# Sparse attention and a top-2 mixture of experts on one core: the ACT and DVE steps of early list parts take their batch's rank, and experts' products are owed 0.7 instead of 1.0 of the attention's time on TensorE

## The chip, the cores and the metric

The kernel runs on one core of a Trainium2 chip. The metric is device time in microseconds of one execution, the median of three. The page and the trace are of one further execution, taken by the hardware profiler.

## The reference, cut to what matters

```python
# attention: 8 batches, 8 heads, 576 tokens, head size 64; heads 0-3 local, 4-7 strided
scores = scale * np.matmul(q, k.transpose(0, 1, 3, 2))
mask_local = (rel >= 0) & (rel < 32)
mask_strided = (rel >= 0) & (pos[None, :] % 32 == pos[:, None] % 32)
attn = softmax(where(masks, scores, -1e9)); x = matmul(attn, v) -> (4608, 512)
# experts: 8 of them, each token goes to the best two
noisy_logits = x @ w_gate + log1p(exp(x @ w_noise)) * noise
top2 = argpartition(-noisy_logits, 2)[:, :2]; top2_w = softmax of the two logits
for e in range(8):
    for k in range(2):
        mask = top2[:, k] == e
        h = np.maximum(x[mask] @ w1[e], 0.0)          # 512 -> 1024
        out[mask] += top2_w[mask, k, None] * (h @ w2[e])   # 1024 -> 512
```

The second half depends on the first through `x`: which tokens an expert gets is known only batch by batch, as the attention of a batch ends and its tokens are routed.

## The kernel before

**Attention.** The work is cut into 32 units, four to a batch: two pairs of strided heads and two of local heads, in turn. A unit transposes k and q on TensorE (L505, L509), forms two score tiles (masks L550, 36 score products at L557), takes the row maxima on DVE (L584) and the exponentials on ACT (L588, L590), transposes these (L598), multiplies by v (L617, L622), scales on DVE (L627 to L646), and transposes the result for the router (L684, L688) while SP stores it to `x_dram` (L663). Evacuations of PSUM go to ACT or DVE, whichever is free sooner (`copy`, L283 to L287).

**Routing.** After the four units of a batch, `route` runs the gate products (L734), softplus, the best two of eight, and the places in the experts' lists (L785 to L798); GpSimd then writes twelve groups of entries to the lists `tab` in DRAM (L824).

**Experts.** An expert's list is worked off in jobs, two or three blocks of 128 tokens at a time. For the first three experts some jobs are cut so that they need only the batches 0 to hb-1 (`SUBS`, hb below 8): these are the *early list parts*. The first needs two batches, the next two need four, then five, and the last three seven. A job loads its list (`tabt`, L925), GpSimd makes indices (`gix`, L982) and gathers the tokens' rows (`xg`, L966), TensorE transposes them (L1008), ACT rounds them to `xhi` (L1019) and DVE takes the remainder `xlo` (L1021). Layer 1 is eight groups of twelve products (L1050), each followed by a ReLU on ACT (`hhi`, L1069) and a remainder on DVE (`hlo`, L1074). Layer 2 is 24 products of 512 columns for each block (L1116), then DVE weighs the result (`prev`, L1141 or L1143) and GpSimd scatters it to the output (L1150). The weights are loaded as `wraw` and split by ACT (L896) and DVE (L897).

**Order.** The program's order is set before it runs, by a planner (`issue_all`). Each piece of work has an engine, an estimated length and a rank. At every step the planner takes, on each engine, the pieces that could start within 120 ns of the first that could, and of these the one of lowest rank. Attention units have ranks 10u; routing comes with its batch; experts' pieces have ranks from ER = 1,000,000 on, so they come last wherever something else could start. `turn(n)` gives a job with hb below 8 the rank 20·2·(hb-1)+20, that of the middle of its last batch. Before the change only the loads of its lists, its weights' loads and its gathers have that rank. Each engine then works its instructions off in the order that the planner left, whatever their real lengths.

**Owing.** While attention is left and an expert's product could run, each attention piece on TensorE adds PACE times its length to `owed`, each expert's product takes its length off. As long as `owed` is positive, TensorE prefers an expert's product that could start within 120 ns. With PACE = 1.0 that aims at equal shares.

Of the kernel before, what the change touches and what calls it, by code (L numbers as in the profile page):

```python
# [22 lines left out]
def kernel(  # L23
# [13 lines left out]
    B, H, S, D = q.shape  # L37
# [169 lines left out]

    GAP = 1500

    PACE = 1.0  # L210

    class Slot:
        def __init__(self, ring=None):
# [57 lines left out]
    def act(n):  # L271
        return 60 + 0.84 * n

    def dve(n):
        return 75 + 1.04 * n
# [15 lines left out]
    def issue_all(expert_banks, t_start):  # L291
# [43 lines left out]
        while ready:  # L335
# [62 lines left out]
            if e == "PE":  # L398
                owed = max(-1500.0, owed - d) if o.expert else min(3000.0, owed + PACE * d) if filler[0] else 0.0
            ready.remove(o)  # L400
# [503 lines left out]
    def experts(zero):  # L904
# [5 lines left out]
        def turn(n):  # L910
            hb = jobs[n][1][3]
            return None if hb == B else 20 * NP * (hb - 1) + 10 * NP
# [77 lines left out]
        def transposes(n, rank):  # L990


            e, (start, nb, tail, hb) = jobs[n]
            xh, xl = R["xhi"].new(), R["xlo"].new()
            XH[n] = (xh, xl)
            for i in range(nb + (tail > 0)):
                xs, rows_of = G_[n][2:]
                xg = xs[i]
                rows = 128 if i < nb else tail
                ng = rows // 32  # L1000
                cols = slice(128 * i, 128 * i + rows)
                if hb < B:
                    xr = Slot()

                    def tr(o, xg=xg, xr=xr):
                        xv = xg.t.rearrange("p g c -> p (g c)").rearrange("p (x c) -> p c x", c=ND)
                        for c in range(ND):
                            nc.tensor.transpose(xr.t[:, 128 * c:128 * c + 128], xv[:, c, :], ident)  # L1008
                    Piece("PE", 108 * ND, tr, rank, read=[xg], psum=xr, expert=True)
                else:  # L1010
                    xr = R["xr"].new()
                    Piece("DVE", 8 * rows, lambda o, xg=xg, xr=xr, ng=ng, rows=rows: nc.vector.transpose(  # L1012
                        xr.t.rearrange("p (c x) -> p c x", c=ND)[:, :, :rows].rearrange("p c (g i) -> p g c i", g=ng),
                        xg.t[:, :ng, :].rearrange("p g (i c) -> p g c i", c=ND)), rank, read=[xg], alloc=[xr], expert=True)
                how = "write" if i else "alloc"

                def view(xr=xr, rows=rows):
                    return xr.t.rearrange("p (c x) -> p c x", c=ND)[:, :, :rows]
                Piece("ACT", act(4 * rows), lambda o, view=view, cols=cols: nc.scalar.copy(  # L1019
                    xh.t[:, :, cols], view()), rank, read=[xr], expert=True, **{how: [xh]})  # L1020
                Piece("DVE", dve(4 * rows), lambda o, view=view, cols=cols: nc.vector.tensor_tensor(  # L1021
                    xl.t[:, :, cols], view(), xh.t[:, :, cols].bitcast(F32), ALU.subtract),
                      rank, read=[xr, xh], expert=True, **{how: [xl]})
                if i + 2 < nb + (tail > 0):

                    xs.append(rows_of(i + 2))
# [3 lines left out]
        def half_used(e):  # L1030
            if e not in counts:
                counts[e] = nc.values_load(over[:1, E + 1 + e:E + 2 + e], engines=[mybir.EngineType.PE], min_val=0,
                                           max_val=NTOK)
            return counts[e]

        def layer1(n, f, rank):
            e, (start, nb, tail, hb) = jobs[n]
            width = nb * 128 + tail
            xh, xl = XH[n]
            whi, wlo = W[1, f]  # L1040
            hh, hl = R["hhi"].new(), R["hlo"].new()
            HT[n, f] = (hh, hl)
            ps = Slot()

            todo = [(d, a, c) for d in range(ND) for a, c in ((whi, xh), (whi, xl), (wlo, xh))]

            def products(which, width):
                for m in which:
                    d, a, c = todo[m]
                    nc.tensor.matmul(ps.t[:, :width], a.t[:, 128 * d:128 * d + 128], c.t[:, d, :width], start=(m == 0),  # L1050
                                     stop=(m == len(todo) - 1))

            def mm(o):
                last = len(todo) - 1
                if not tail:
                    return products(range(last + 1), width)

                products([0], width)
                with tc.If(half_used(e) > tail // 2) as used:
                    products(range(1, last), width)  # L1060
                with used.Else():
                    with tc.If(half_used(e) > 0) as some:
                        products(range(1, last), width - tail // 2)
                    with some.Else():
                        products(range(1, last), width - tail)
                products([last], width)
            Piece("PE", 12 * (width / 2.4 + 2.5), mm, rank, read=[xh, xl, whi, wlo], psum=ps, expert=True,
                  after=lengths_known if tail else [])
            Piece("ACT", act(width) + 30, lambda o: nc.scalar.activation(hh.t[:, :width], ps.t[:, :width], AF.Relu), rank,  # L1069
                  read=[ps], alloc=[hh], expert=True)  # L1070
            main = nb * 128

            def low(dst, c0, c1):
                nc.vector.scalar_tensor_tensor(dst, ps.t[:, c0:c1], 0.0, hh.t[:, c0:c1].bitcast(F32), op0=ALU.max,  # L1074
                                               op1=ALU.subtract)

            def lows(o):
                low(hl.t[:, :main], 0, main)
                if tail:

                    low(hh.t[:, width:width + tail], main, width)
            Piece("DVE", dve(main) + (dve(tail) if tail else 0), lows, rank, read=[ps, hh], write=[hh] if tail else [],
                  alloc=[hl], expert=True)
# [15 lines left out]
        def layer2(n, i, rank, pv):  # L1099
# [39 lines left out]
            def weighted(o):  # L1139
                if first:  # L1140
                    nc.vector.tensor_scalar(pv.t, ps.t, tb.t[:, i, 1:2].bitcast(F32), None, op0=ALU.mult)  # L1141
                for r in () if first else range(0, 2 * rows if half else rows, rows):
                    nc.vector.scalar_tensor_tensor(pv.t[:rows, :], ps.t[r:r + rows, :], tb.t[:rows, i, 1:2].bitcast(F32),  # L1143
                                                   pv.t[:rows, :], op0=ALU.mult, op1=ALU.add)
            Piece("DVE", (1 + half) * dve(512), weighted, rank, expert=True,
                  **({"read": [ps, tb], "alloc": [pv], "after": zero[:-(-known // ZC)]} if first else
                     {"read": [ps, tb, pv], "write": [pv]}))
# [13 lines left out]
        for i in range(NF):  # L1161
            W[1, i] = weights_of(jobs[0][0], 1, i, ER, turn(0))
        W2[0] = [weights_of(jobs[0][0], 2, i, ER, turn(0)) for i in range(NF)]
        transposes(0, ER)
        for n, (e, (start, nb, tail, hb)) in enumerate(jobs):
            nb += tail > 0
            others = [x for y in range(E) if y != e for x in out_done[y]]
            rank = ER + 100 * n
            change = n + 1 < NJOB and jobs[n + 1][0] != e
            pvs = {i: previous(n, i, rank, others) for i in range(min(2, nb))}  # L1170
            if n + 1 < NJOB:
                gather(n + 1, rank + 1)
            for f in range(NF):
                layer1(n, f, rank + 2)
            if change:
                for i in range(NF):
                    W[1, i] = weights_of(jobs[n + 1][0], 1, i, rank + 20, turn(n + 1))
            if n + 1 < NJOB:
                transposes(n + 1, rank + 3)
            for i in range(nb):  # L1180
                layer2(n, i, rank + 4 + i, pvs[i])
                if i + 2 < nb:
                    pvs[i + 2] = previous(n, i + 2, rank + 4, others)
            if n + 1 < NJOB:
                W2[n + 1] = W2[n]
                if change:
                    W2[n + 1] = [weights_of(jobs[n + 1][0], 2, i, rank + 21, turn(n + 1)) for i in range(NF)]
# [17 lines left out]
    for u in range(NU):  # L1205
        rank = 10 * u
# [92 lines left out]
```

## Time and profile before

| | |
|---|---|
| three executions | 1097.59, 1098.72, 1097.29 us; median 1097.59 |
| the profiled execution | 1092.48 us, of which the span from first to last instruction is 1090.8 us |
| instructions | 23344, of them 8645 matmul records |
| DVE, ACT, POOL busy | 606.2, 434.4, 544.1 us |
| gate products of the eight batches begin at | 43.8, 76.3, 110.9, 142.2, 171.8, 221.2, 271.1, 324.4 us |

Times in the text are us from the start of the span. A row of a view by stretches names the stretch and its length, and for each engine its busy time and, in brackets, the number of instructions; PEld is the loading of weights into TensorE, PEclk the granted clock as a share of full speed. "Busy" of PE counts modelled ends of pipelined matmuls.

### The profile page before, as it was taken

The numbers are of one execution on the slowest core, as the hardware profiler recorded it, in microseconds if no ns is written. First come the engines' busy times: TensorE is split into PE (matmuls) and PEld (weight loads), VectorE is DVE, ScalarE is ACT, GpSimd is POOL, SyncE is SP. The second block draws the span as 40 slices with busy tenths as digits, with TensorE's granted clock in tenths as the row PEclk, the third lists the DMA queues.
The fourth block names the chain that finished last, engine by engine and source line by source line (L and its number), as shares of the span: only waits on it lengthen the run. The fifth ranks groups of instructions, "written<-read, shape, count | busy, mean of one in ns | idle before, by whom it ended". The sixth has DMA issues, their size and how long they took to land.

```text
span 1090.8 us, 23344 instructions
## 1 busy us (share of the span) xinstructions
PE 1058.4 (97%) x8645; PEld 933.9 (86%) x8645; DVE 606.2 (56%) x1614; ACT 434.4 (40%) x1123; POOL 544.1 (50%) x730
## 2 busy tenths in 40 slices
PE   8888899999999999999999999999999999999995
PEld 7776679888898899889998989898988898898994
DVE  7779896687655235647663455345534653374341
ACT  6789986666653112314331233123311331142120
POOL 1045353434425455656666546564646465647520
PEclk8999999999999999999999999999999999999998
DMA  8889999889454323535553245224522452243210
GB/s 178 206 179 234 231 217 232 222 228 269 132 168 116 100 87 98 152 115 174 171 177 93 71 116 177 79 62 131 163 76 69 126 166 74 78 144 107 73 57 23
DMA packets 169163, 151.89 MB, mean 139 GB/s; under 512 B 52588, under 2 KB 137068, under 8 KB 169029
## 3 DMA queue, kind: packets, MB, share of 16 engines
q1 hardware_dynamic: 145028, 92.30, 33.8%
q0 software_dynamic: 24000, 57.82, 17.4%
q8 instruction: 82, 1.34, 0.5%
q14 instruction: 53, 0.43, 0.1%
HBM read 111.72 MB, written 39.39 MB: 139 GB/s over the span
## 4 chain that ended last, share of the span: by engine, by line
PE 89%; DVE 4%; ACT 3%; DMA 2%; issue 1%; POOL 0%; POOLq 0%; DVEq 0%; ACTq 0%; SPq 0%
PE bankA L1116 6%; PE bankH L1116 6%; PE bankA L1050 5%; PE bankD L1116 5%; PE bankG L1116 5%; PE bankB L1050 5%; PE bankH L1050 5%; PE bankE L1050 5%; PE bankD L1050 5%; PE bankG L1050 5%; PE bankB L1116 5%; PE bankE L1116 4%; PE bankF L1050 4%; PE bankC L1050 4%; PE bankC L1116 4%; PE bankF L1116 3%
## 5 line engine op out<-in xcount | busy, mean ns | idle before, releaser
L973 POOL DMA_INDIRECT xg<-x_dram,gxx x240 | 240.4, 1002 | 111.7 <-issue 56.7
L1150 POOL DMA_INDIRECT out_dram<-prev,tabt x80 | 81.5, 1019 | 104.1 <-DVE prev L1143 51.2
L824 POOL DMA_INDIRECT tab<-ent,addr x96 | 93.1, 970 | 74.8 <-issue 24.7
L1092 POOL DMA_INDIRECT prev<-out_dram,gix x76 | 73.3, 964 | 85.8 <-issue 30.2
L1012 DVE STREAM_TRANSPOSE xr<-xg 128x512 f32<-128x512 f32 (+1 forms) x64 | 66.4, 1038 | 18.1 <-DMA xg<-x_dram,gxx 16.1
L1019 ACT CAST xhi<-xr 128x512 fp32r<-128x512 f32 (+1 forms) x64 | 37.8, 591 | 71.6 <-DVE xr L1012 71.6
L896 ACT CAST w2hi<-wraw 128x512 fp32r<-128x512 f32 x80 | 47.3, 618 | 28.1 <-PE bankC L1125 7.4
L897 DVE TENSOR_TENSOR w1lo<-wraw,w1hi 128x512 fp32r<-128x512 f32 x80 | 54.8, 689 | 2.9 <-ACT w1hi L896 0.5
L897 DVE TENSOR_TENSOR w2lo<-wraw,w2hi 128x512 fp32r<-128x512 f32 x80 | 52.7, 687 | 1.6 <-ACT w2hi L896 1.3
L1021 DVE TENSOR_TENSOR xlo<-xr,xhi 128x512 fp32r<-128x512 f32 (+1 forms) x64 | 42.1, 658 | 18.4 <-ACT xhi L1019 17.2
L896 ACT CAST w1hi<-wraw 128x512 fp32r<-128x512 f32 x80 | 48.8, 614 | 0.1
L812 POOL COPY ent<-wt 96x12 f32<-96x12 f32 x8 | 1.6, 197 | 88.1 <-DVE wt L806 88.1
L1050 PE MATMUL bankA<-xhi,w1hi 128*128 128x256 f32 (+3 forms) x140 | 42.3, 302 | 0.0
L1050 PE MATMUL bankA<-xhi,w1lo 128*128 128x256 f32 (+3 forms) x140 | 41.6, 297 | 0.0
L1069 ACT ACTIVATE hhi<-bankB 128x256 fp32r<-128x256 f32 (+2 forms) x33 | 14.1, 426 | 69.0 <-PE bankB L1050 68.9
L1050 PE MATMUL bankA<-xlo,w1hi 128*128 128x256 f32 (+3 forms) x140 | 41.5, 296 | 0.0
L1050 PE MATMUL bankB<-xhi,w1hi 128*128 128x256 f32 (+3 forms) x132 | 40.2, 304 | 0.0
L1050 PE MATMUL bankH<-xhi,w1hi 128*128 128x256 f32 (+3 forms) x132 | 40.0, 303 | 0.0
L1050 PE MATMUL bankE<-xhi,w1hi 128*128 128x256 f32 (+3 forms) x132 | 39.6, 300 | 0.0
L1050 PE MATMUL bankB<-xhi,w1lo 128*128 128x256 f32 (+3 forms) x132 | 39.4, 298 | 0.0
L1050 PE MATMUL bankH<-xhi,w1lo 128*128 128x256 f32 (+3 forms) x132 | 39.4, 298 | 0.0
L1050 PE MATMUL bankB<-xlo,w1hi 128*128 128x256 f32 (+3 forms) x132 | 39.3, 297 | 0.0
(669 smaller groups left out, 3565.6 us busy)
## 6 DMA issues: line engine op xcount, KB each, us to landing
wraw<-in_moe_w_dram SPq DMA_DIRECT2D x160, 256.0 KB
out_dram<-zeros SPq DMA_DIRECT2D x12, 768.0 KB
ks<-in_k_dram SPq DMA_DIRECT2D x15, 320.0 KB
qs<-in_q_dram SPq DMA_DIRECT2D x15, 320.0 KB
vraw<-in_v_dram SPq DMA_DIRECT2D x30, 160.0 KB
raw<-in_k_dram SPq DMA_DIRECT2D x16, 288.0 KB
v_l<-in_v_dram SPq DMA_DIRECT2D x16, 288.0 KB
raw<-in_q_dram SPq DMA_DIRECT2D x16, 288.0 KB
```

Source lines behind the costliest of these rows:

```text
L824: st = nc.gpsimd.indirect_dma_start(out=tab, out_offset=bass.IndirectOffsetOnAxis(ap=s["addr"].t[:, t, kk:kk + 1], axis=0), in_=s["ent"].t ...
L896: Piece("ACT", act(512) + 30, lambda o: nc.scalar.copy(hi.t, raw.t), rank, read=[raw], alloc=[hi], expert=True)
L897: Piece("DVE", dve(512), lambda o: nc.vector.tensor_tensor(lo.t, raw.t, hi.t.bitcast(F32), ALU.subtract), rank, read=[raw, hi], alloc=[lo] ...
L973: dma(lambda o, g=g: nc.gpsimd.indirect_dma_start(out=xg.t[:, g, :], out_offset=None, in_=x_dram[:4 * known, :], in_offset=bass.IndirectOf ...
L1012: Piece("DVE", 8 * rows, lambda o, xg=xg, xr=xr, ng=ng, rows=rows: nc.vector.transpose(xr.t.rearrange("p (c x) -> p c x", c=ND)[:, :, :row ...
L1019: Piece("ACT", act(4 * rows), lambda o, view=view, cols=cols: nc.scalar.copy(xh.t[:, :, cols], view()), rank, read=[xr], expert=True, **{h ...
L1021: Piece("DVE", dve(4 * rows), lambda o, view=view, cols=cols: nc.vector.tensor_tensor(xl.t[:, :, cols], view(), xh.t[:, :, cols].bitcast(F ...
L1050: nc.tensor.matmul(ps.t[:, :width], a.t[:, 128 * d:128 * d + 128], c.t[:, d, :width], start=(m == 0), stop=(m == len(todo) - 1))
L1069: Piece("ACT", act(width) + 30, lambda o: nc.scalar.activation(hh.t[:, :width], ps.t[:, :width], AF.Relu), rank, read=[ps], alloc=[hh], ex ...
L1092: dma(lambda o: nc.gpsimd.indirect_dma_start(out=pv.t[:rows, :], out_offset=None, in_=out[:known, :], in_offset=bass.IndirectOffsetOnAxis( ...
L1116: nc.tensor.matmul(ps.t, HT[n, f][p[0]].t[:, cols], W2[n][f][p[1]].t, start=(m == 0), stop=(m == len(todo) - 1))
L1150: st = nc.gpsimd.indirect_dma_start(out=out[:known, :], out_offset=bass.IndirectOffsetOnAxis(ap=tb.t[:rows, i, 0:1], axis=0), in_=pv.t[:ro ...
```

## The change

Four places of the planner's input change. PACE goes from 1.0 to 0.7. For jobs with hb below 8, `transposes` gives the transposes on TensorE and the steps `xhi` and `xlo` the rank `turn(n)`; `layer1` gives that rank to the ReLU and the remainder `hlo`, not to the products; `layer2` gives it to the weighing and to the output scatter on GpSimd. Nothing else changes: the same instructions run on the same data, in another order, and with another choice of ACT or DVE for some evacuations (13 more on ACT, 13 fewer on DVE).

```diff
-    PACE = 1.0
+    PACE = 0.7
...
             xh, xl = R["xhi"].new(), R["xlo"].new()
             XH[n] = (xh, xl)
+            rank = rank if hb == B else turn(n)
             for i in range(nb + (tail > 0)):
...
             Piece("PE", 12 * (width / 2.4 + 2.5), mm, rank, read=[xh, xl, whi, wlo], psum=ps, expert=True,
                   after=lengths_known if tail else [])
+            rank = rank if hb == B else turn(n)
             Piece("ACT", act(width) + 30, lambda o: nc.scalar.activation(hh.t[:, :width], ps.t[:, :width], AF.Relu), rank,
                   read=[ps], alloc=[hh], expert=True)
...
+            rank = rank if hb == B else turn(n)
             Piece("DVE", (1 + half) * dve(512), weighted, rank, expert=True,
```

Line numbers of the changed kernel are one to three higher from L996 on (L1008 becomes L1009, L1021 L1022, L1050 L1051, L1074 L1076, L1150 L1153).

**DVE, the second `xlo` of the first early part.** Before, 70 rows stand between the first `xlo` and this one:

```order
L286 COPY aT<-bankC 96x512
L286 COPY qT_s<-qT_s 64x4x8
L286 COPY xT<-bankA 128x512
L286 COPY aT<-bankD 96x512
L627 TENSOR_SCALAR rs<-bankB 128x4
L286 COPY aT<-bankG 96x128
L632 RECIPROCAL rs<-rs 128x4
L1021 TENSOR_TENSOR xlo<-bankF,xhi 128x4x128
L638 TENSOR_TENSOR xo_139<-bankB,rs 128x4x64
```

Now ten rows stand between the two:

```order
L584 TENSOR_REDUCE mx<-bankF 128x5
L1022 TENSOR_TENSOR xlo<-bankE,xhi 128x4x128
L627 TENSOR_SCALAR rs<-bankG 128x4
L629 TENSOR_SCALAR rs<-bankG 64x2
L286 COPY v_s_135<-vraw 72x8x64
L632 RECIPROCAL rs<-rs 128x4
L634 RECIPROCAL rs<-rs 64x2
L287 TENSOR_SCALAR qT_l<-bankH 128x96x3
L638 TENSOR_TENSOR xo_138<-bankG,rs 128x4x64
L646 TENSOR_TENSOR xo_138<-bankG,rs 64x128
L286 COPY aT<-bankC 72x512
L1022 TENSOR_TENSOR xlo<-bankE,xhi 128x4x128
```

Sixty rows of attention and routing that stood between the two now come behind both.

**PE, behind the first transposes of gathered rows (`xg`).** Before, attention follows, up to the scores of the 21st unit; only the second transposes stand in it, behind the gate products of batch 3. The first layer-1 product comes 194 rows further down:

```order
L1008 MATMUL bankE<-ident,xg 128x128 x4
L617 MATMUL bankG<-v_l_133,aT 64x65 x8
L622 MATMUL bankG<-v_l_133,aT 64x65 x2
L505 MATMUL bankH<-ident,ord 128x96 x3
L598 MATMUL bankD<-ident,ex 72x128 x4
L509 MATMUL bankB<-ident,qs 128x72 x4
L509 MATMUL bankC<-ident,ks 128x72 x4
L509 MATMUL bankH<-ident,qs 128x72 x4
L598 MATMUL bankA<-ident,ex 72x128 x4
L617 MATMUL bankF<-v_s_134,aT 64x65 x8
```

Now the second transposes and the first layer-1 products stand within the same unit:

```order
L1009 MATMUL bankE<-ident,xg 128x128 x4
L617 MATMUL bankG<-v_l_133,aT 64x65 x8
L622 MATMUL bankG<-v_l_133,aT 64x65 x2
L505 MATMUL bankH<-ident,ord 128x96 x3
L509 MATMUL bankD<-ident,qs 128x72 x4
L509 MATMUL bankB<-ident,ks 128x72 x4
L598 MATMUL bankC<-ident,ex 72x128 x4
L1009 MATMUL bankE<-ident,xg 128x128 x4
L598 MATMUL bankH<-ident,ex 72x128 x4
L688 MATMUL bankA<-ident,xo_138 128x128 x4
L617 MATMUL bankF<-v_s_134,aT 64x65 x8
L1051 MATMUL bankG<-xhi,w1hi 128x256
```

From here to the 32nd unit's scores the products are spread anew. Counted in the two orders, with the units told by their score products: between the scores of the 17th and the 24th unit stood 96 products of layer 1 and 36 of layer 2, and now stand 108 and 48; between those of the 24th and the 32nd stood 192 and 108, and now stand 180 and 54. What is missing there comes later, in a row with the other experts' products, whose order is the same as before.

**POOL, around the gather of the parts that need four batches.** Before:

```order
L824 DMA tab<-ent,addr 39936x3
L810 COPY ent<-tokid 96x12
L811 COPY ent<-xrow 96x12
L812 COPY ent<-wt 96x12
L823 MEMSET spacer 1x1
L824 DMA tab<-ent,addr 39936x3
L823 MEMSET spacer 1x1
L824 DMA tab<-ent,addr 39936x3
L982 TENSOR_SCALAR gix<-tabt 128x2 x2
L966 DMA xg<-x_dram,gix 128x512 x2
```

Now:

```order
L824 DMA tab<-ent,addr 39936x3
L1153 DMA out_dram<-prev,tabt 1152x512
L810 COPY ent<-tokid 96x12
L811 COPY ent<-xrow 96x12
L812 COPY ent<-wt 96x12
L982 TENSOR_SCALAR gix<-tabt 128x2 x2
L966 DMA xg<-x_dram,gix 128x512 x2
```

An output scatter has come in ahead of the gather, and two entry scatters of batch 4 have gone behind it.

## The prediction

> **What bounds the kernel now.** First the page: busy time, the slices, the chain that ended last.
>
> ```profile
> PE 1058.4 (97%) x8645; PEld 933.9 (86%) x8645; DVE 606.2 (56%) x1614; ACT 434.4 (40%) x1123; POOL 544.1 (50%) x730
> ...
> PE   8888899999999999999999999999999999999995
> ...
> PE 89%; DVE 4%; ACT 3%; DMA 2%; issue 1%; POOL 0%; POOLq 0%; DVEq 0%; ACTq 0%; SPq 0%
> ```
>
> TensorE is the bound nearly throughout, and its work is the same before and after. So the change can only move the time in which TensorE waits or runs thinly. Where that is, the view by stretches says; I cut it at the first score products of the 17th, 21st, 24th and 32nd unit.
>
> ```profile
> core 0: us, PE busy (x) PEld busy (x) DVE busy (x) ACT busy (x) POOL busy (x), PEclk, DMA share, GB/s
> 0.00:133.80 133.80, 116.02 (x1837) 92.63 (x1841) 107.27 (x438) 106.91 (x329) 37.78 (x98) 0.92 0.92 206
> 133.80:163.20 29.40, 26.70 (x477) 21.53 (x471) 27.77 (x117) 24.93 (x84) 15.88 (x32) 1.00 0.98 213
> 163.20:204.70 41.50, 41.50 (x533) 36.46 (x529) 26.85 (x112) 27.43 (x77) 19.72 (x39) 1.00 0.97 240
> 204.70:303.20 98.50, 98.50 (x1243) 85.50 (x1239) 69.77 (x259) 63.34 (x187) 40.51 (x72) 1.00 0.78 203
> ...
> 340.00:1060.00 720.00, 720.00 (x4194) 648.80 (x4193) 349.20 (x613) 194.56 (x406) 413.77 (x468) 1.00 0.39 114
> 1060.00:1090.80 30.80, 18.86 (x114) 16.34 (x113) 4.27 (x9) 2.31 (x6) 3.78 (x4) 0.85 0.08 28
> ```
>
> From 163 us to about 1060 PE is busy without a hole. Up to 133.8 it isn't, but there the order is unchanged; the tail is unchanged too. What the change can touch is 133.8 to 303 us and the rest of the attention behind it. The stretch 133.8 to 163.2 has a hole (26.70 of 29.40) and DVE at 27.77 of 29.40, 94%. No experts' products run there, as the next rows show: the score products (36 to a unit), layer 1, layer 2, in the three stretches.
>
> ```profile
> 133.80:163.20 29.40, 3.67 (x146) 3.39 (x148) 1.00 0.98 213
> 163.20:204.70 41.50, 2.67 (x111) 2.54 (x115) 1.00 0.97 240
> 204.70:303.20 98.50, 7.34 (x292) 6.77 (x292) 1.00 0.78 203
> ```
> ```profile
> 133.80:163.20 29.40, 0.00 (x0) 0.00 (x0) 1.00 0.98 213
> 163.20:204.70 41.50, 13.26 (x96) 11.80 (x96) 1.00 0.97 240
> 204.70:303.20 98.50, 26.51 (x192) 23.56 (x192) 1.00 0.78 203
> ```
> ```profile
> 163.20:204.70 41.50, 9.93 (x36) 6.31 (x36) 1.00 0.97 240
> 204.70:303.20 98.50, 29.67 (x108) 18.96 (x108) 1.00 0.78 203
> ```
>
> So 4, 3 and 8 units of attention (146, 111 and 292 over 36) stood beside 0, 132 and 300 products. Why they began so late, the timeline shows:
>
> ```profile
> 144.15 0.68 PE L1008 MATMUL bankF<-ident,xg 128*128 128x128 f32 x4
> 146.13 0.59 ACT L1019 CAST xhi<-bankF 128x512 fp32r<-128x512 f32 x1
> 163.41 0.66 DVE L1021 TENSOR_TENSOR xlo<-bankF,xhi 128x512 fp32r<-128x512 f32 x1
> 164.20 0.36 PE L1050 MATMUL bankE<-xhi,w1hi 128*128 128x256 f32 x1
> 164.40 0.28 PE L1050 MATMUL bankE<-xlo,w1hi 128*128 128x256 f32 x1
> 165.57 0.27 PE L1050 MATMUL bankE<-xhi,w1lo 128*128 128x256 f32 x1
> ...
> 187.23 0.39 PE L1116 MATMUL bankE<-w2lo,hhi 128*128 128x512 f32 x1
> 188.16 0.40 PE L1116 MATMUL bankE<-w2hi,hlo 128*128 128x512 f32 x1
> ```
>
> The second block was transposed at 144, rounded by 146.7, and then its remainder stood on DVE behind attention until 163.4. The first product follows 0.8 us later.
>
> **The change, part by part.** *Ranks.* Both `xlo` now stand early in DVE's order, and the first products come ahead of the 18th unit's scores, some 20 us sooner by the rows above. Nothing is added: the same steps, the same products. *PACE.* The early products are spread over more units. By the counts of the two orders, the 15 units from the 17th to the 32nd score products hold 288 products of layer 1 in both kernels, and 102 of layer 2 where 144 stood.
>
> The prices: from the second to the twelfth product of a layer-1 group 164.40 to 165.57, 1.17 us in ten steps, 0.117 each; layer 2 from 187.23 to 188.16, four steps, 0.233 each. All 288 early products are of this width. Taken off, they leave what the attention itself cost:
>
> - 133.8 to 163.2: 29.4 us for 4 units, 7.35 each;
> - 163.2 to 204.7: 96 × 0.117 = 11.2 and 36 × 0.233 = 8.4, so 41.5 - 19.6 = 21.9 for 3 units, 7.3 each;
> - 204.7 to 303.2: 22.5 and 25.2, so 98.5 - 47.7 = 50.8 for 8 units, 6.35 each.
>
> Together 102.1 us for 15 units, 6.81 each. The few transposes of gathered rows stay in these numbers, since both orders have nearly the same. The 42 products of layer 2 that leave the stretch are done later at the same 0.233, where PE is full, so they cost nothing in sum. **The change is therefore 15a - 102.1**, with a the attention's cost of a unit in the new order.
>
> The lower bound of a is 6.35, the best row: 95.3, a gain of 6.8. The upper is 7.35, the row without products: 110.3, a loss of 8.2. Between them I make two estimates. By products: the new order puts 288 × 0.117 + 102 × 0.233 = 57.5 us beside 15 units, 3.8 to a unit. From 7.35 at none to 6.35 at 47.7/8 = 6.0, a straight line gives 6.71, a gain of 1.4. By DVE's load: the three stretches hold 27.77 + 26.85 + 69.77 = 124.4 us of DVE; two weighings fewer change little; in 102 + 57.5 = 160 us that is 77%, between 71% (69.77 of 98.5) at 6.35 and 94% at 7.35. The line gives 6.61, a gain of 2.9. If 3.8 us of products already fill a unit's holes, the gain is the full 6.8. I take a = 6.6: 99.0, **a gain of 3.1 us**. That is nearest to the estimate by DVE, since DVE was what the first products waited for. The unit after the 32nd scores is left at no change.
>
> *GpSimd.* The output scatters of the first early part now stand ahead of the gathers for the parts of four batches. They have to be issued (1.02 us each) and wait for `prev`.
>
> ```profile
> L1150 POOL DMA_INDIRECT out_dram<-prev,tabt x80 | 81.5, 1019 | 104.1 <-DVE prev L1143 51.2 <-issue 22.3 <-DVE w1lo L897 7.1
> ```
> ```profile
> POOL out_dram L1150 <- DVE prev L1143: 51.2, 34, 8.8
> ```
> ```profile
> 187.28 1.04 POOL L966 DMA_INDIRECT xg<-x_dram,gix  x1 [0.28 <-POOL gix L982]
> ...
> 195.48 0.69 PE L1008 MATMUL bankD<-ident,xg 128*128 128x128 f32 x4
> ```
>
> Before, 8 us lie between the gather's issue and the transposes that use it, and two entry scatters have left the way. So 1 us for the scatter is hidden; a wait as long as the longest above, 8.8, would not quite be. I cost it at nothing and keep it as a rival.
>
> The Trainium skill's "Perfetto Trace Analysis", section "Identifying the Most-Contended Engine", says that busy time of matmuls is a bad measure of TensorE's headroom and that the busy time of weight loads is a better one. By the first measure the stretch from 133.8 has 29.40 - 26.70 = 2.7 us to win; by the second, 21.53 of 29.40 (73%) against 85.50 of 98.50 (87%), it has some 4.7. The trace agrees with the rule as far as the unit times go, 4 × (7.35 - 6.35) = 4.0.
>
> **Sum.** The profiled execution took 1092.48 (span 1090.8), so it would take 1089.4. The median of the three runs, 1097.59, lies 5.1 above it; the same difference there gives **1094.5**.
>
> **The rivals.**
>
> *Given back (about no change).* Products only move from later units to earlier ones; if holes are filled in proportion to products, the line of 6.71 holds, and a between 6.66 and 6.95 leaves the time within 2.2 us. For it: the middle stretch had 6.5 us of products to a unit and still cost 7.3. Against it: that stretch holds the first part's start, with a wait for its own data. The case that the change does nothing it says belongs here; the order shows otherwise.
>
> *DVE waits in line (slower).* DVE works in order. A remainder `hlo` that stands early waits there for its ReLU, and the attention's steps behind it wait too. The waits of DVE from 160 to 340 us show the price:
>
> ```profile
> DVE hlo L1074 <- ACT hhi L1069: 13.8, 12, 2.9
> ```
>
> That is 1.15 us a time in 12 of these. With the new rank, `hlo` comes straight behind its ReLU in all 24 groups (288 over 12): 24 × 1.15 = 27.6, that is 13.8 more. DVE then has 124.4 + 13.8 in 160 us plus its former waits, 95% when both are counted, and a goes to 7.35: 8.2 us slower, 1105.8. It decides above a = 6.81, at about half of that added wait. Against it: while DVE stands, products of other groups can run, up to four banks of them.
>
> The Trainium skill speaks for this rival: "TensorE: Matmul & The Clock Gate", section "Architectural detail: the array is 16× 32×32, not 1× 128×128", calls the queues of ScalarE and VectorE strictly first in, first out. The row of waits agrees.
>
> *The gather comes late (slower).* If the output scatter waits 8.8 us and the gather's issue with it, the transposes wait about 4 us beyond the 8 us of slack less landing, and TensorE, in order, with them: 1094.5 + 4 = 1098.5, or 1102 if it comes twice.
>
> **How the numbers follow.** Forecast, a from 6.35 to 6.66, a gain of 2.2 to 6.8: 0.45. A still larger gain, if the spread helps the middle stretch beyond the best row: 0.03. Given back, within 2.2 us: 0.30. DVE in line: 0.14, a late gather: 0.08. Measured runs of this kernel can tell 0.2%, 2.2 us, from no change. So faster 0.48, same 0.30, slower 0.22. The range goes from 1090 (a = 6.3) to 1102 (a = 7.1); each end leaves out about a tenth.
>
> **What would show it.** Right: the first layer-1 products begin at 140 to 146 us rather than 164; the stretch of the 17th to 21st unit has PE busy near its length; gate products of batch 4 begin a few us later than 171.8, those of batch 7 some 10 us earlier than 324.4, since about 10 us of products have left; no PE wait on transposes near 195 us. Wrong: `hlo` waiting for `hhi` over 20 us in the attention, DVE over 90% behind 163 us, PE idle again behind 163 us, or half clock there (PEclk was 1.00 from 133.8 on). If units cost 6.8 or more, the forecast falls at that step.

## The result, and the profile after

The changed kernel takes 1090.64 us, the median of 14 runs (1085.82 to 1096.07). The kernel before, run beside it, takes 1097.2 us. The ratio is 0.9942, with an interval of 0.9928 to 0.9955: faster by 0.58%, some 6.4 us, where 3.1 us were forecast. Two later executions of the kernel before, of 2059 us each, are left out of all numbers below. The profiled execution of the changed kernel is one of its slower ones, 1093.69 us (span 1091.9), and so even 1.2 us longer than that of the kernel before. Whole spans of the two profiles therefore tell nothing; the stretches do.

The page of the changed kernel: busy time, the granted clock in 40 slices, the chain that ended last.

```profile
PE 1058.5 (97%) x8645; PEld 937.4 (86%) x8645; DVE 606.9 (56%) x1601; ACT 433.7 (40%) x1136; POOL 547.3 (50%) x730
...
PE   8888899999999999999999999999999999999995
...
PEclk8898999999999999999999999999999999999998
...
PE 89%; DMA 4%; DVE 3%; ACT 3%; issue 1%; POOL 0%; POOLq 0%; SPq 0%; DVEq 0%; ACTq 0%
```

Read over the whole span, nothing has moved: TensorE is the bound, with the same busy time to 0.1 us, and its first five slices have holes, as before. 0.58% of the span is a quarter of one slice.

The view by stretches of the changed kernel, cut at the same four units as before (the first score products of the 17th, 21st, 24th and 32nd unit):

```profile
core 0: us, PE busy (x) PEld busy (x) DVE busy (x) ACT busy (x) POOL busy (x), PEclk, DMA share, GB/s
0.00:139.80 139.80, 118.72 (x1833) 95.47 (x1837) 107.28 (x438) 106.58 (x328) 37.80 (x98) 0.90 0.85 197
139.80:180.70 40.90, 40.87 (x599) 36.90 (x594) 33.06 (x126) 30.70 (x98) 20.96 (x42) 1.00 0.96 223
180.70:210.70 30.00, 29.56 (x441) 24.89 (x437) 21.89 (x99) 21.96 (x70) 11.70 (x20) 1.00 0.94 241
210.70:293.50 82.80, 82.80 (x1165) 73.23 (x1161) 66.77 (x241) 61.86 (x192) 37.09 (x70) 1.00 0.90 229
```

The first row is code that the change doesn't touch, and it took 6.0 us longer (139.80 against 133.80), at a lower clock (0.90 against 0.92). That is where the slow profile comes from. Behind it, the way from the 17th to the 32nd scores is 153.7 us instead of 169.4. The stretch with the hole is full now: PE 40.87 of 40.90, PEld 90% of it where it was 73%, and DVE 81% where it was 94%.

The experts' products in the last three stretches, layer 1 and then layer 2, in the same view for one line each (PE, PEld):

```profile
139.80:180.70 40.90, 13.32 (x96) 11.81 (x96) 1.00 0.96 223
180.70:210.70 30.00, 1.66 (x12) 1.47 (x12) 1.00 0.94 241
210.70:293.50 82.80, 24.93 (x180) 22.09 (x180) 1.00 0.90 229
```
```profile
139.80:180.70 40.90, 4.91 (x18) 3.16 (x18) 1.00 0.96 223
180.70:210.70 30.00, 8.27 (x30) 5.25 (x30) 1.00 0.94 241
210.70:293.50 82.80, 14.82 (x54) 9.46 (x54) 1.00 0.90 229
```

With the prediction's prices (0.117 and 0.233 us a product) the attention is left with 40.9 - 11.2 - 4.2 = 25.5 us for 4 units, 6.37 each; 30.0 - 1.4 - 7.0 = 21.6 for 3 units, 7.20 each; 82.8 - 21.1 - 12.6 = 49.1 for 8 units, 6.14 each. Together 96.2 for 15 units, 6.41 each, where it was 6.81. So 5.9 us have gone: 4 × 0.98 = 3.9 from the first four units, 0.3 from the middle three, 8 × 0.21 = 1.7 from the last eight. Behind the 32nd scores about 1.0 us comes back: from there to the end the profile of before needs 787.6 us and this one 798.4, 10.8 more, of which the 42 products of layer 2 that moved there explain 9.8. From the 17th scores to the end it is 952.1 us instead of 957.0, a gain of 4.9 in these two executions beside some 6.4 in the medians.

The timeline shows the early start. First DVE, then PE:

```profile
142.52 0.69 DVE L1022 TENSOR_TENSOR xlo<-bankE,xhi 128x512 fp32r<-128x512 f32 x1
145.34 0.69 DVE L1022 TENSOR_TENSOR xlo<-bankE,xhi 128x512 fp32r<-128x512 f32 x1
```
```profile
146.04 0.39 PE L1051 MATMUL bankG<-xhi,w1hi 128*128 128x256 f32 x1
146.27 0.28 PE L1051 MATMUL bankG<-xlo,w1hi 128*128 128x256 f32 x1
```

The second `xlo` is done at 146.03, and the first product starts at once, 6.2 us behind the 17th scores. Before, it started 30.4 us behind them (164.20 against 133.80).

### The profile page after: what moved, and what is told of

Its sections match the earlier page's. It is cut to its first block, busy times and chain, and to the rows that moved or that the text cites. A ratio compares the mean times of both kernels' runs of the same rounds, so it can differ in the third digit from the quotient of the medians.

```text
span 1091.9 us, 23351 instructions
## 1 busy us (share of the span) xinstructions
PE 1058.5 (97%) x8645; PEld 937.4 (86%) x8645; DVE 606.9 (56%) x1601; ACT 433.7 (40%) x1136; POOL 547.3 (50%) x730
## 4 chain that ended last, share of the span: by engine, by line
PE 89%; DMA 4%; DVE 3%; ACT 3%; issue 1%; POOL 0%; POOLq 0%; SPq 0%; DVEq 0%; ACTq 0%
PE bankB L1118 6%; PE bankE L1118 6%; PE bankD L1118 5%; PE bankD L1051 5%; PE bankF L1051 5%; PE bankG L1051 5%; PE bankH L1051 5%; PE bankC L1051 5%; PE bankB L1051 5%; PE bankG L1118 5%; PE bankA L1051 5%; PE bankA L1118 4%; PE bankE L1051 4%; PE bankC L1118 4%; PE bankH L1118 4%; PE bankF L1118 4%
## 5 line engine op out<-in xcount | busy, mean ns | idle before, releaser
L1153 POOL DMA_INDIRECT out_dram<-prev,tabt x80 | 82.5, 1032 | 111.8 <-DVE prev L1145 52.6
L1013 DVE STREAM_TRANSPOSE xr<-xg 128x512 f32<-128x512 f32 (+1 forms) x64 | 66.5, 1038 | 13.8 <-DMA xg<-x_dram,gxx 12.6
L1022 DVE TENSOR_TENSOR xlo<-xr,xhi 128x512 fp32r<-128x512 f32 (+1 forms) x64 | 42.2, 659 | 18.4 <-ACT xhi L1020 17.2
L1051 PE MATMUL bankD<-xhi,w1hi 128*128 128x256 f32 (+3 forms) x136 | 41.0, 302 | 0.0
L1071 ACT ACTIVATE hhi<-bankG 128x256 fp32r<-128x256 f32 (+2 forms) x33 | 14.0, 423 | 67.9 <-PE bankG L1051 67.9
L1051 PE MATMUL bankF<-xhi,w1hi 128*128 128x256 f32 (+3 forms) x136 | 40.6, 299 | 0.0
L1051 PE MATMUL bankD<-xhi,w1lo 128*128 128x256 f32 (+3 forms) x136 | 40.5, 298 | 0.0
L1051 PE MATMUL bankD<-xlo,w1hi 128*128 128x256 f32 (+3 forms) x136 | 40.4, 297 | 0.0
L1051 PE MATMUL bankF<-xhi,w1lo 128*128 128x256 f32 (+3 forms) x136 | 40.1, 295 | 0.0
L1051 PE MATMUL bankG<-xhi,w1hi 128*128 128x256 f32 (+3 forms) x132 | 39.9, 303 | 0.0
L1051 PE MATMUL bankF<-xlo,w1hi 128*128 128x256 f32 (+3 forms) x136 | 39.9, 294 | 0.0
L1051 PE MATMUL bankG<-xhi,w1lo 128*128 128x256 f32 (+3 forms) x132 | 39.2, 297 | 0.0
L1051 PE MATMUL bankG<-xlo,w1hi 128*128 128x256 f32 (+3 forms) x132 | 39.0, 296 | 0.0
```

The costliest lines, as they stand in the source:

```text
L1153: st = nc.gpsimd.indirect_dma_start(out=out[:known, :], out_offset=bass.IndirectOffsetOnAxis(ap=tb.t[:rows, i, 0:1], axis=0), in_=pv.t[:ro ...
```

## The experiments

The theory: the gain is filled holes, and it needs both halves of the change. Early ranks start the first part's products sooner; the thinner share makes them last until the next part is there. The rivals: one half alone gives the gain; or the clock gives it, as the slow first row suggests.

All edits are to the changed kernel unless said otherwise. "Cost of a unit" is worked out as above, in us, with the products of layer 1 and layer 2 in each stretch in brackets. Ratios are to the kernel before, run beside.

| kernel | ratio and interval | units 17 to 21 | 21 to 24 | 24 to 32 | all 15 |
|---|---|---|---|---|---|
| before | 1 | 7.35 (0, 0) | 7.3 (96, 36) | 6.35 (192, 108) | 6.81 |
| after | 0.9942 [0.9928, 0.9955] | 6.37 (96, 18) | 7.20 (12, 30) | 6.14 (180, 54) | 6.41 |
| e4, the same again | 0.9955 [0.9938, 0.9972] | 6.37 (96, 18) | 7.00 (12, 30) | 6.14 (180, 54) | 6.37 |
| e1, ranks alone | 0.9992 [0.9971, 1.0013] | 6.92 (96, 36) | 7.47 (0, 12) | 6.56 (252, 96) | 6.84 |
| e2, PACE alone | 1.0008 [0.9985, 1.0031] | 8.70 (0, 0) | 7.52 (96, 18) | 5.95 (132, 78) | 6.99 |
| e3, PACE and first rank | 0.9988 [0.9967, 1.001] | 6.46 (96, 12) | 6.70 (12, 36) | 6.95 (180, 60) | 6.77 |
| e5, without the third rank | 0.9954 [0.9936, 0.9972] | 6.47 (96, 18) | 7.07 (12, 30) | 6.17 (180, 54) | 6.43 |
| e6, PACE 0.5 | 0.9989 [0.9963, 1.0016] | 6.22 (96, 0) | 6.76 (0, 48) | 6.67 (168, 48) | 6.57 |
| e7, PACE 0.85 | 0.994 [0.9916, 0.9964] | 6.58 (96, 30) | 6.40 (12, 18) | 6.52 (180, 90) | 6.51 |

The last four columns are of one profiled execution each, the ratio of 7 to 14 runs. In e1, 60 of the 252 products are 384 columns wide instead of 256; the trace has them 0.173 us apart (298.80 to 300.53 in ten steps), and that is the price taken for them.

What lies ahead of the 17th scores differs between these executions by up to 7.4 us, so the time from there to the end tells the kernels apart better than the span: 957.0 us before; 952.1 after, 951.5 in e4, 953.9 in e5, 952.9 in e7; but 956.9 in e1, 957.5 in e3, 961.6 in e2 and 962.0 in e6. That is the same grouping as by the ratios.

**e1: the ranks alone.**

```diff
-    PACE = 0.7
+    PACE = 1.0
```

> The new ranks with PACE back at 1.0. In its order the first part's products are used up by the 23rd unit's scores (96 and 48), and the next part's begin behind the 24th: two or three units between have none. Theory A (a unit that has some products beside it costs about 6.4 us, one without costs 7.35; the time goes by how many units have some): 12 or 13 units of 15 at 6.4 and 2 or 3 at 7.35, a gain of 3 to 4 us of the 6.6, so a ratio of 0.9965 to 0.997 to the kernel before. Theory B (the holes fill in proportion to products): 1.5a - line with 5 us to a unit, a gain of 4 us, and it matters nothing where they stand. Theory C (the ranks do nothing, the lower share does it): ratio 1.000.

No gain that can be told from none, where theories A and B both expected 3 to 4 us. The first two stretches of e1, from the 17th to the 24th scores:

```profile
134.10:181.40 47.30, 46.58 (x635) 40.75 (x631) 34.23 (x132) 31.54 (x100) 23.55 (x45) 1.00 0.99 241
181.40:206.60 25.20, 22.93 (x358) 18.88 (x354) 18.71 (x83) 19.09 (x61) 8.92 (x17) 0.93 0.88 210
```

At the full share the first four units eat 96 and 36 products; 12 are left for the next three. There the hole comes back (22.93 of 25.20), and the clock falls to 0.93. The hole has moved from the 17th unit to the 21st, as "Given back" had it.

**e2: PACE alone.** On the kernel before:

```diff
-    PACE = 1.0
+    PACE = 0.7
```

> PACE 0.7 with the ranks of before. The products still begin behind the 21st unit's scores, so four units stay without. Theory A: 11 units at 6.4 rather than at 6.6, a gain of 0 to 2 us, ratio 0.998 to 1.000. Theory B: fewer products beside the attention (228 and 96 where 288 and 144 stood), a loss of 1 to 2 us, ratio 1.001 to 1.002. Theory C: ratio 0.994, the whole gain.

No gain either: up to the 21st unit the order is that of the kernel before, so the hole stays. It even cost 34.8 us in this execution, where the profile of before has 29.4. The same stretch, cut where the clock changes:

```profile
135.10:154.60 19.50, 16.23 (x309) 13.12 (x303) 16.96 (x77) 16.21 (x52) 10.13 (x21) 1.00 1.03 251
154.60:164.80 10.20, 10.20 (x115) 8.73 (x113) 7.04 (x27) 5.20 (x19) 4.20 (x8) 0.50 0.66 144
164.80:169.90 5.10, 4.05 (x67) 3.39 (x67) 4.30 (x14) 4.40 (x17) 2.89 (x5) 0.99 0.86 185
```

For 10.2 us TensorE has half its clock, and there it is the bound at once (10.20 of 10.20). At 0.50 it does in 10.2 us what takes 5.1; 34.8 - 5.1 is 29.7, near the 29.4 in the profile of before. So an unfilled stretch costs 7.35 a unit at the full clock and 8.7 with a spell like this. The last eight units, beside 132 and 78 products, are the cheapest of the table, 5.95.

**e3: PACE and the rank of `transposes` alone** (the rank lines in `layer1` and `layer2` taken out).

```diff
             Piece("PE", 12 * (width / 2.4 + 2.5), mm, rank, read=[xh, xl, whi, wlo], psum=ps, expert=True,
                   after=lengths_known if tail else [])
-            rank = rank if hb == B else turn(n)
...
-            rank = rank if hb == B else turn(n)
             Piece("DVE", (1 + half) * dve(512), weighted, rank, expert=True,
```

> PACE 0.7 and the new rank only for the transposes and the steps xhi and xlo; ReLU, hlo, weighing and scatter keep their old rank. The order spreads the products nearly as the full change does. If the early xlo is what the ranks bring: ratio 0.994 as the full change, within 0.002. If the early ReLU and hlo (banks free sooner) carry part of it: 0.996 or above.

The early start is there, and the first seven units are as cheap as after the change. The last eight cost 6.95. Of e3, that stretch, and the longest wait of TensorE in it:

```profile
202.60:293.20 90.60, 88.48 (x1175) 77.56 (x1171) 67.39 (x240) 62.83 (x195) 40.23 (x72) 0.96 0.86 226
```
```profile
PE bankG L1009 <- DMA xg<-x_dram,gix: 2.1, 1, 2.1
```

PE waits 2.1 us for gathered rows, and PEclk is 0.96: about 90.6 × 0.04 = 3.6 us lost. That would make 5.7 of the 6.5 us by which this stretch is dearer than after the change (8 × 0.81). Whether every execution of e3 loses it in this way stays open: see e12.

**e4: the changed kernel once more**, beside e1 to e3.

> The changed kernel once more, on the chip of the three others: ratio 0.994, as measured before. In the profile the 15 units from the 17th to the 32nd scores cost 6.3 to 6.5 us each beside the products.

The gain repeats, and so do the rows: of e4, the first and the third stretch.

```profile
135.90:176.80 40.90, 40.87 (x595) 36.90 (x592) 33.02 (x126) 30.72 (x98) 20.77 (x42) 1.00 0.97 223
206.20:289.00 82.80, 82.80 (x1167) 73.22 (x1161) 66.62 (x241) 61.74 (x192) 37.37 (x70) 1.00 0.91 230
```

40.90 and 82.80 us, as in the first profile, though what lies ahead took 135.9 us here and 139.8 there. In these two executions what the change decides is the same; what differs lies ahead of it.

**e5: without the rank of the weighing and the output scatter.**

```diff
-            rank = rank if hb == B else turn(n)
             Piece("DVE", (1 + half) * dve(512), weighted, rank, expert=True,
```

> The full change without the rank of the weighing and of the output scatter. The products stand nearly as in the full change. If the ReLU and hlo are what the run with xlo alone lacked (there the last eight units cost 6.95 beside the products, with the full change 6.14): 6.1 to 6.3 for those units and ratio 0.995. If it is the weighing and the scatter: 6.8 or more and ratio 0.998. If that run's 6.95 was one stall of its own order: 6.1 to 6.5 as well.

The whole gain is there without it (0.9954). The third rank brings nothing that can be measured. By the ratios the second, of the ReLU and `hlo`, is then what e3 lacked, though the two intervals just overlap (0.9967 and 0.9972). How it helps is not shown: the 6.17 of the last eight units fits the theory of `hlo` as well as that of one stall in e3.

**e6 and e7: the share.**

```diff
-    PACE = 0.7
+    PACE = 0.5
```

> The new ranks with PACE 0.5. Every unit from the 18th on has some products and the attention ends earlier; 264 and 96 products stand beside it. Theory A (some products are enough): a stays at 6.4, ratio 0.994 as with 0.7. Theory B (in proportion): a rises to 6.6 or more, ratio 0.997. No unit is without products, so no half clock behind the 17th unit.

With PACE = 0.85 in its place:

> The new ranks with PACE 0.85, between 0.7 and the 1.0 that gained nothing. The first part is used up by the 24th unit's scores, about one unit goes without. Theory of the hunger behind the first part: one third of the loss seen with 1.0, ratio 0.995 to 0.997, units 21 to 24 at 7.2 to 7.4. If products per unit alone cost (dense units wait for banks): units 17 to 21 at 6.6 to 6.9.

0.85 does as well as 0.7, and the hunger expected at its units 21 to 24 did not come (6.40). At 0.5 the gain is gone in the median, though the runs spread from 1090.0 to 1103.2 us. Half clock came twice behind the 17th scores of its profile, for 3.4 us at 222 and 6.8 us at 338, where the expectation had none. Of e6: the longest wait for gathered rows, its place in the timeline, and the stretch behind the 32nd scores.

```profile
PE bankF L1009 <- DMA xg<-x_dram,gix: 3.3, 1, 3.3
```
```profile
339.73 1.13 PE L1009 MATMUL bankF<-ident,xg 128*128 128x128 f32 x4 [3.25 <-DMA xg<-x_dram,gix]
```
```profile
289.60:350.00 60.40, 57.15 (x398) 49.85 (x390) 27.97 (x91) 17.91 (x44) 33.54 (x55) 0.94 0.53 138
```

In this execution, with fewer products beside it, the attention runs ahead of the lists. TensorE comes to the transposes of a late part 3.25 us before its rows have landed, waits in order, and runs the stretch at a clock of 0.94. From the 17th scores to the end this execution of e6 (1101.51 us, 5 above its median) needs 962.0 us, that of the changed kernel 952.1, of the kernel before 957.0.

**e8: the clock held up.** Products of zeros (`warm`, which the kernel has) are put into gaps of 0.23 us and more that the planner leaves on TensorE while no expert's product could run. The trace shows 74 of them (8719 matmul records where the changed kernel has 8645). This is added work: the bank that they write is overwritten by the next piece.

```diff
+            if e == "PE" and o.psums and not o.expert and not filler[0]:
+                for i in range(min(4, int((t - now["PE"]) // 230))):
+                    nc.tensor.matmul(o.psums[0].t[:, :256], warm[:, :128], warm, start=True, stop=True)
             last = o.fn(o)
```

> The full change with 82 products of zeros added in the first half of the attention, where the order leaves TensorE a gap of 0.23 us or more; they are written to the bank that the next piece overwrites. If idle stretches let the clock fall there (PEclk 0.90 up to the 17th unit) and the clock is what sets these executions' spread: PEclk 0.95 or more up to the 17th unit, that unit 2 to 5 us earlier, ratio 0.990 to 0.993. If TensorE's clock isn't what bounds that stage (DVE and ACT are): no gain or up to 5 us slower, ratio 0.995 to 0.999.

1086.27 us (1085.23 to 1088.16, 6 runs), ratio 0.991 [0.9884, 0.9935]: 10 us below the kernel before, and 3 to 4 below e7 and e5 on the same chip. Of e8, the first 127.9 us:

```profile
0.00:127.90 127.90, 111.27 (x1818) 88.69 (x1822) 101.19 (x420) 100.20 (x312) 33.12 (x91) 0.99 0.91 200
```

PEclk is 0.99 where the first stretch has 0.90 after the change and 0.92 before. The units from the 17th to the 32nd scores cost 6.42, as without the zeros, so the gain isn't there. Nor does this execution show it ahead of them: its 17th scores come at 133.8 us, earlier than in the first profile and e4 (139.8 and 135.9), but no earlier than in the profile of before (133.8), e7 (133.8) or e5 (132.4), and at 1087.9 us it is one of e8's slower ones. Where the 3 to 4 us come from stays open.

**e9: the zeros on the kernel before; e10: with PACE 0.85; e11: up to 8 of them in gaps of 0.13 us and more.** The traces show 85, 74 and 166 zeros. The edit is that of e8, in e11 with `min(8, int((t - now["PE"]) // 130))`.

> The kernel before with the same kind of products of zeros (93 of them, some of these between the 17th and the 21st unit). If the change's gain and the clock are separate: 4 to 5 us gained by the clock alone, ratio 0.9955 to 0.9965, and the units 17 to 21 still at 7.0 or more. If a good part of the change's gain came from half clock that it ends between units 17 and 21: 0.992 to 0.994, and those units at 6.4 to 6.8.

> The new ranks, PACE 0.85 and the products of zeros. Both gains together: ratio 0.989 to 0.991, as with 0.7 or 1 to 2 us better.

> The full change with 174 instead of 82 products of zeros, in gaps from 0.13 us. The clock was at 0.99 already, so there is nothing more to win: PEclk 0.99 to 1.00 and ratio 0.991 to 0.993. If the added products begin to stand in the attention's way: 0.994 or more, the 17th unit later than 134 us.

In this set every kernel took 3% longer, the kernel before too (1130.07 us, 21 runs), nearly all of it in the attention. One difference stands out in the four traces of the set: up to 1060 us TensorE stands idle 20 to 24 times, 9.2 to 12.5 us in sum, with nothing in the profile to wait for ("issue"), where the ten other traces have this at most twice. The cause of that was not found. Within the set e9 has a ratio of 0.9969 [0.9943, 0.9995], e10 0.9922 [0.9894, 0.995], e11 0.9942 [0.9917, 0.9968]. So the zeros alone bring about 0.3%, and with a change of PACE and ranks about 0.8%, near the 0.991 of e8. More of them brought no more that can be told: e11's 0.9942 is that of the change without zeros. They don't fill the holes between the 17th and the 21st scores, where a unit of e9 costs 9.48, and they don't always hold the clock: of e9, a stretch ahead of the first products.

```profile
141.10:154.80 13.70, 12.09 (x123) 10.48 (x123) 8.55 (x27) 7.22 (x22) 5.21 (x11) 0.50 0.78 188
```

**e12: e3 once more**, one execution.

> A second look at the kernel with the new rank for xlo alone and PACE 0.7. If its last eight units cost 6.95 because of its order: 6.8 to 7.1 again, with a wait of transposes for a gather. If that was one execution's late transfer: 6.1 to 6.4, and no such wait.

1129.38 us beside 1130.07. Its last eight units cost 7.92, with no wait on gathered rows among the long ones. That is neither of the two forecasts: in this set units were dearer throughout (7.07 to 9.48 in the stretches of the four profiles), so this doesn't decide what e3 lost. It stays open how much of it is the gather's wait. A kernel with the rank of `layer1` alone was not tried.

## Why the prediction was right, and where its size was off

**The mechanism** came as written. The first products start 6.2 us behind the 17th scores, the hole is gone, and the cost of 15 units fell. e1 and e2 show that neither half does it alone. One step was missing: the prediction names only the two `xlo` as what the ranks bring. e3 has these and the new share, its first products begin 6.8 us behind the 17th scores, and its ratio is 0.9988; with the rank of the ReLU and `hlo` (e5) it is 0.9954.

**The size: the term a.** The prediction took a = 6.6 between 6.35 and 7.35, by a line in DVE's load; a second line, in products, gave 6.71. Measured: 6.41 in the first profile and 6.37 in e4, so 15a - 102.1 is -5.9 and -6.5 where -3.1 was forecast. Both lines failed at the same step. A unit's holes are not filled in proportion: four units with 15.4/4 = 3.9 us of products cost 6.37, as much as the eight of before with 6.0 us. Beyond some 3 us more products even made these first four units dearer: 6.22 at 2.8 us (e6), 6.37 at 3.9, 6.58 at 4.6 (e7), 6.92 at 4.9 (e1). The sentence "if 3.8 us of products already fill a unit's holes, the gain is the full 6.8" held, nearly. Among the last eight units thinner was cheaper too, with e7 out of line: 6.56 in e1 with (192 × 0.117 + 60 × 0.173 + 96 × 0.233)/8 = 6.9 us, 6.35 before with 6.0, 6.52 in e7 with 5.3, 6.14 after with 4.2, 5.95 in e2 with 4.2. In e3 and e6, which had half clock in this stretch, they cost 6.95 with 4.4 and 6.67 with 3.9. So the lower bound, the "best row", was not the floor for these either. Only the middle three units kept their price (7.20 and 7.00), at 8.4/3 = 2.8 us of products; since e7 has 6.40 there at 1.9, the load isn't the reason, and it stays open. The term that was put at nothing, the rest behind the 32nd scores, cost 1.0 us.

**Given back** did not occur with the thinner share. e1 is that rival: with PACE 1.0 the hole moves on by four units.

**DVE waits in line** fell. The waits of DVE of the changed kernel, 139.8 to 293.5 us (in all, times, longest):

```profile
DVE hlo L1076 <- ACT hhi L1071: 6.9, 7, 2.4
```

Before, between the same units (133.8 to 303.2 us):

```profile
DVE hlo L1074 <- ACT hhi L1069: 7.0, 5, 2.9
```

The prediction's 13.8 us in 12 times were counted from 160 to 340 us, so they belong to more than the 24 groups that it multiplied them by. That rival forecast 13.8 us more; in these two executions the early rank of `hlo` costs DVE no wait.

**The gather comes late** fell, though its wait came. GpSimd of the changed kernel in the timeline, and then PE:

```profile
187.88 1.16 POOL L1153 DMA_INDIRECT out_dram<-prev,tabt  x1 [6.37 <-DVE prev L1143]
...
195.73 0.20 POOL L812 COPY ent<-wt 96x12 f32<-96x12 f32 x1 [6.36 <-DVE wt L806]
...
196.80 1.04 POOL L966 DMA_INDIRECT xg<-x_dram,gix  x1 [0.27 <-DVE kT_s L286]
```
```profile
203.36 0.65 PE L1009 MATMUL bankD<-ident,xg 128*128 128x128 f32 x4
```

The scatter waits 6.37 us for `prev`; but then GpSimd waits again, 6.36 us, for the weights from batch 4's routing. The gather doesn't need these, but in both orders it stands behind the copy that does. The routing is last, not the scatter, and the transposes wait for nothing. "I cost it at nothing" was right, for a reason that the prediction didn't give.

**What it said of the clock** was wrong. "PEclk was 1.00 from 133.8 on" is true of that one execution: e2 runs the same order there and has 10.2 us at half clock. **The offset** of 5.1 us between profile and median, carried over to the changed kernel, had no ground either: there the profile is 3.05 us above the median. Differences between stretches carry over; the place of one execution among its kin doesn't.

**The signs.** The gate products of batch 4 came 10.3 us later, counted from the 17th scores (188.1 - 139.8 against 171.8 - 133.8), and those of batch 7 21.7 earlier (308.7 and 324.4): the directions are right, both sizes about double.

## What to carry to other kernels

Where a stage that waits on latencies can be filled with other work, price its unit at two or three loads before drawing a line: here 3 to 4 us a unit filled it as well as 6 did. Early work needs a supply that lasts: start it sooner and spread it thinner together, since either alone moved the hole or left it, and spread too thin (0.5) the gain was gone; in the one execution traced the stage outran the data it waits for next. Compare two kernels by stretches that the change touches, and look at the same code ahead of it to see what one execution is worth.

## What the runs showed of the hardware

Ahead of the kernel's tail, TensorE's clock halves in spells of 3.4, 6.8, 10.2, 13.7 or, once (e12), 17.1 us, in stretches where TensorE is busy most of the time. Ahead of the spell in e2 it was busy for 16.23 of 19.50 us, and its longest single wait there was 1.5 us. The Trainium skill, "TensorE: Matmul & The Clock Gate", section "HAM oscillation — how this bites in real kernels", warns of idle gaps above some 3.4 us; by that rule there should be no spell here, and the trace does not bear it out. Its section "A second HAM failure mode: psum-queue depth-cycling" says that frequent short idles between groups of products suffice; the e2 rows agree with that. One spell, in e9 at 113.8 us, does follow a wait of 3.6 us.

The 3.4 us just ahead tell more than the longer stretch. Of e2:

```profile
151.20:154.60 3.40, 1.75 (x36) 1.27 (x26) 3.19 (x29) 2.54 (x9) 0.22 (x2) 1.00 1.01 239
```

TensorE was busy for 1.75 of 3.40 us. Within one execution the spells begin and end on a grid of 3.413 us. Cut into windows on that grid, the first 600 us of the fourteen traces give one picture. Behind a window at full clock in which PE was busy for less than half, half clock followed each time (16 of 16); behind one with 50 to 80% in 45 of 184; behind one with 80% or more never (0 of 2139). Half clock ended only behind a window with 95% or more (61 of 76, and none of the 31 below). So in these traces the clock goes with the busy share of single windows, mostly without a long gap.

The clock also tells most executions of one kernel apart. Over 57 executions of the kernel before mean clock and time have a correlation of -0.79, with 7.2 us for 0.01 of the clock. It does not explain the change: the mean clock is 0.984 over the 14 runs of the changed kernel, and 0.983 over those 57; side by side on one chip it is 0.9825 in e4 and 0.9835 in the kernel before. Added work can win time, and the clock rises with it: e8 has a mean clock of 0.994 and takes 3 to 4 us less than e5 and e7 with 0.984; e9 has 0.984 and takes 3.1 us less than the kernel before with 0.974. By the slope each should have won some 7 us. The zeros gave half of it, so either they cost some, or the slope holds other causes as well.
